# Two zero fills on ScalarE, a third behind the wide patterns, and the wide distances behind the first pattern, in an attention and channel-mix kernel

## The chip, the core and the metric

The kernel runs on one NeuronCore of a Trainium2 chip: TensorE (PE) multiplies matrices, VectorE (DVE), ScalarE (ACT) and GpSimd (POOL) do elementwise work, and SyncE (SP) issues the DMA transfers. The metric is the device time of one launch in microseconds. Before the change it was 506.46 us, the median of three runs (506.25, 506.46 and 509.65).

## What is computed

Attention over 4 batches, 8 heads, 768 positions and 64 features, with a window of `n_local` = 96 keys and `n_global` = 8 keys that all may see, and a linear bias by distance; its output goes through a channel mix of two matrix products and a gate.

```python
scores = (q @ k^T) / sqrt(64) - slope[h] * dist      # slope[h] = 2 ** -(h + 1)
dist   = n_local where the key is global and not local, else |i - j|
a      = softmax(scores where the key is global or local, else -1e9)
x      = a @ v                                       # (4, 768, 512)
xk, xr = mu * x + (1 - mu) * x_prev                  # x_prev: one position earlier
out    = sigmoid(xr @ w_r) * (relu(xk @ w_k) ** 2 @ w_v)
```

## The kernel before

**Tiles.** A tile is 128 queries of one batch, all 8 heads: 24 tiles, 6 per batch. A tile's scores are made two heads at a time (`scores`, hp = 0 to 3, PSUM tiles `s_0` to `s_3`, two buffers). The first tile of a batch sees its own 128 keys. Any other sees 104 earlier keys as well (8 global ones, then the 96 before it), 232 in all. DVE adds the bias pattern to the scores and finds the largest in the same instruction (L366), ACT takes the exponential and its sum (L367), DVE makes the reciprocal (L373, L374), POOL or ACT scales (L380, L378), PE transposes (L392), ACT copies to SBUF (L394), and PE multiplies by v two tiles later in the program (L411).

**The native tiles.** The first six tiles use 128-partition operands of which only the lower 64 partitions hold data; the upper 64 are zeroed once (L261 to L271). There are two query buffers (`qz`) and a ring of three key buffers (`kz`), so five fills of 64x1024 on POOL. Tile 0 needs query 0 and key 0; tile 1 query 1, key 1 and key 0; tile 2 key 2 too. `first_keys` (L274) copies the batch's 8 global keys out of key buffer 0 (`k_first`), and, for tile 1, writes them over a strip of key buffer 0 that tile 1's L357 reads. That write waits until tile 0's scores have read the buffer.

**The patterns.** `pat0` (8 heads of 128x128) is the bias of a batch's first tile, `pat` (8 heads of 128x232) that of all others. Both come from distances that DVE computes from iota values and the two sizes, which a DMA brings: L118 to L128 make `dist0`, the six L132 on DVE and two L134 on POOL scale it per head, L137 to L140 make the wide `dist`, four L144 on ACT and four L146 on POOL scale that. L693 to L698 (`okf`) test whether the sizes fit this path.

**The weights.** Ten slabs of 1 MB come as 64-bit words. DVE packs each to 32 bits (L174 to L176), ACT rounds it to a high half (L178), and for the first six PE makes the rest (L188, L189), which ACT copies (L190). Channel-mix work (`kp`, `z`, `vps`) is fed into the PE stream a few matmuls at a time.

**What sets the order.** Each engine runs its own stream in order. The streams' order is made when the program is built, by a scheduler that simulates a timeline, so an edit to one engine's work can shift neighbours on others. All large loads go through SP's one queue; a load waits there for its buffer, and what stands behind it waits too. Ten matmuls on zeros (L95) stand at the head of PE's stream.

Of the kernel before, what the change touches and what calls it, by code (L numbers as in the profile page):

```python
# [25 lines left out]
GMAX = 8  # L26
# [15 lines left out]
def tile_biased_attention_channel_mix(ctx: ExitStack, tc: tile.TileContext, qT, kT, v, n_sizes, mu_kr, w_k, w_v, w_r, q_rows, k_rows, v_rows, slopes, out):  # L42
# [94 lines left out]
    vec.tensor_scalar(local[:, 0:96], flts[:, 0:96], nlf, FAR, op0=ALU.is_ge, op1=ALU.mult)  # L137
    vec.tensor_copy(dist[:, OWN:W], local[:, 96:224])
    vec.tensor_scalar(dist[:, 0:GMAX], glo[:, 0:GMAX], nlf, None, op0=ALU.max)
    vec.tensor_add(dist[:, GMAX:OWN], local[:, 0:96], flts[:, 0:96])  # L140
    for h in range(H):
        c = -8.0 * 2.0 ** -(h + 1)
        if h % 2:
            act.mul(pat[:, h, :], dist, c)  # L144
        else:
            pool.tensor_scalar(pat[:, h, :], dist, c, 1.0, op0=ALU.mult, op1=ALU.mult)  # L146
# [3 lines left out]
    w_raw, w_live, w_done = {}, {}, {}  # L150

# [6 lines left out]
    def weight_load(i):  # L158


        raw = w_raw[i] = const.tile([128, 1024, 2], I32, tag=f"w{i}", name=f"w64_{i}")
        tc.keep_in_program_order(weight_words(i, raw))

    def weight_begin(i):


        name, src, j = w_steps[i]
        raw = w_raw.pop(i)
        a = p4k.tile([128, 1024], I32, tag="t4k", name=f"wa_{i}")
        low, top = raw[:, :, 0], raw[:, :, 1]  # L170

        vec.tensor_scalar(a, top, 3, 0x3FFFFFF8, op0=ALU.logical_shift_left, op1=ALU.bitwise_and)  # L174
# [3 lines left out]
        act.copy(both[:, 0, :], a.bitcast(F32))  # L178
        w_live[i] = a, both
        w_done[i] = both  # L180

    def weight_end(i):
        name, src, j = w_steps[i]
        a, both = w_live.pop(i)
        if name in 'kr':
            for o in (0, 512):
                rest = ps_f.tile([128, 512], F32, name=f"rest_{i}_{o}", tag="f")
                pe.matmul(rest, ident, a.bitcast(F32)[:, o : o + 512], start=True, stop=False)  # L188
                pe.matmul(rest, minus, both[:, 0, o : o + 512], start=False, stop=True)  # L189
                act.copy(both[:, 1, o : o + 512], rest)  # L190
        else:
            vec.tensor_sub(both[:, 1, :], a.bitcast(F32), both[:, 0, :])
        for k in range(1 if name == "k" else 2):
# [65 lines left out]


    q_zero, k_ring = [], []  # L261
# [12 lines left out]
    def first_keys(n):  # L274
        if n % NT:
            pool_copy(state[n - 1]["kr"][0:64, :, 128 - OWN : 128 - BACK], k_first)
        else:
            pool_copy(k_first, state[n]["kr"][0:64, :, 0:GMAX])

    def load_tile(n):  # L280
# [12 lines left out]
        for o in halves:  # L293
            nc.sync.dma_start(qr[o : o + 64], qT[n])
        for o in halves:
# [9 lines left out]
    def load_v(n):  # L305

        b, t = divmod(n, NT)
        va = v_pool.tile([128, DM], F32, name=f"va_{n}", tag="va")
# [36 lines left out]
    def scores(n, hp):  # L345
# [16 lines left out]
        for u in range(2):  # L362
            h = 2 * hp + u
            o = ps[:, u * 256 : u * 256 + w]
            e = e_pool.tile([128, W], F32, name=f"e_{n}_{h}", tag="e")
            vec.tensor_tensor_reduce(out=e[:, :w], in0=o, in1=p[:, h, :], op0=ALU.add, op1=ALU.min, scale=-0.125, scalar=3.0e38, accum_out=s["nmax"][:, h : h + 1])  # L366
            act.activation(e[:, :w], e[:, :w], AF.Exp, bias=s["nmax"][:, h : h + 1], scale=-1.0, accum_out=s["sum"][:, h : h + 1])  # L367
            s["e"][h] = e
        if hp % 2 == 0:
            return  # L370
# [4 lines left out]
        for u in range(nh):  # L375
            e = s["e"][h0 + u]
            if n < 6 and u < 1:
                act.mul(e[:, :w], e[:, :w], r[:, u : u + 1])  # L378
# [3 lines left out]
    def transposes(n, hp):  # L382
# [10 lines left out]
        for k, p in enumerate(parts):  # L393
            act.copy(et[0:p, k * 256 : k * 256 + 256], pt[0:p, k * 256 : k * 256 + 256])  # L394
        s["et", hp] = et

    def weighted(n, hp):
# [14 lines left out]
        if hp == 3:  # L412
# [8 lines left out]
            xt = state["x", c]  # L421
            act.copy(xt[:, :, 1 + 128 * i : 129 + 128 * i], s["av"].rearrange("p (a q) -> p a q", a=4))  # L422

# [5 lines left out]
    def mix(xc, xp, tag, tmp_pool, out_pool, on_act=False):  # L429
# [9 lines left out]
        act.copy(hi, tmp)  # L439
        vec.tensor_sub(lo, tmp, hi)  # L440
        return hi, lo
# [62 lines left out]
    def ffn(c):  # L504
        xt = state["x", c]
        xk = mix(xt[:, :, 1:257], xt[:, :, 0:256], "k", p4k, f_pool, c == 0)
        xr = mix(xt[:, :, 1:257], xt[:, :, 0:256], "r", p4k, f_pool, c == 0)
# [3 lines left out]
    LAG = 3  # L511
    queue = []
    budget = [0.0]
# [14 lines left out]
    for step in range(NTILES + 1):  # L528
# [6 lines left out]
        for hp in range(4):  # L535
# [9 lines left out]
            if hp == 0:  # L545
                if step >= LAG and (step - LAG) % 2 == 0:
                    queue.append(ffn((step - LAG) // 2))
                    if len(queue) == 1 and step == LAG:
                        budget[0] = -17.5
            run_ffn(2.5)  # L550
# [3 lines left out]
            slot = 4 * step + hp  # L554
            weights_load(W_LOADS[min(slot, len(W_LOADS) - 1)])
            n = W_BEGUN[min(slot, len(W_BEGUN) - 1)]
            weights_go(n, n - 1 if slot < len(W_BEGUN) else n)
    for i in range(4):
# [133 lines left out]
    wide_i = const.tile([1, 1], I32, name="wide_i")  # L692
    vec.tensor_scalar(okf[:, 0:1], nlf, float(LMAX), None, op0=ALU.is_le)  # L693
    vec.tensor_scalar(okf[:, 1:2], nlf, 1.0, None, op0=ALU.is_ge)
    vec.tensor_mul(okf[:, 0:1], okf[:, 0:1], okf[:, 1:2])
    vec.tensor_scalar(okf[:, 1:2], ngf, float(GMAX), None, op0=ALU.is_le)
    vec.tensor_mul(okf[:, 0:1], okf[:, 0:1], okf[:, 1:2])
    vec.tensor_scalar(okf[:, 0:1], okf[:, 0:1], -1.0, 1.0, op0=ALU.mult, op1=ALU.add)  # L698
    vec.scalar_tensor_tensor(okf[0:1, 0:1], worst[0:1, 1:2], 256.0, okf[0:1, 0:1], op0=ALU.is_gt, op1=ALU.max)
# [49 lines left out]
```

## Time and profile before

| | |
|---|---|
| median of three runs | 506.46 us |
| the profiled execution | 507.19 us |
| its span, first to last instruction | 505.4 us |
| PE busy | 495.7 us (98%) |
| DVE, ACT, POOL busy | 352.9, 344.8, 233.1 us |
| mean granted clock of PE | 0.988 of full |

The profile is of one execution. The span leaves out 1.8 us around the program. Times in the rows below are counted from the span's start. A matmul's end is modelled, so PE's waits are best read from where its next instruction starts, and from the view of waits.

### The profile page before, as it was taken

To read this page: it belongs to the slowest core of one execution; us is meant where nothing else is said; L and a number is where in the kernel's file an instruction comes from. 1 tells how busy PE (TensorE), PEld (TensorE's weight loads), DVE (VectorE), ACT (ScalarE), POOL (GpSimd) and SP (SyncE) were. 2 spreads that over 40 slices of the span, in tenths; PEclk is the share of its full clock that TensorE was granted. 3 is DMA by queue.
4 is the path that set the end of the run, shared out by engine and by line. 5 is a ranking of instruction groups with operands and counts; after the bars stand their busy time and mean duration, and the time that the engine had idled before them with its cause. 6 is when DMAs were issued, how large, how long until landed. Compare 5 with 4: busy or idle time off the path is not lost.

```text
span 505.4 us, 10334 instructions
## 1 busy us (share of the span) xinstructions
PE 495.7 (98%) x3608; PEld 435.4 (86%) x3608; DVE 352.9 (70%) x842; ACT 344.8 (68%) x857; POOL 233.1 (46%) x374
## 2 busy tenths in 40 slices
PE   6999999999999999999999999999999999999996
PEld 3767998998998998898898898898898898897985
DVE  6897979968678668658768658758768755457441
ACT  4799878577577577666577677667577678587360
POOL 7552438546546535527547536528447435204000
PEclk8799999999999999999999999999999999999999
DMA  8997361633503603513512513513423215647311
GB/s 240 323 236 252 106 184 38 163 85 83 165 22 92 176 18 85 144 58 79 152 38 82 156 51 80 150 55 81 130 61 79 84 41 163 207 155 263 127 41 48
DMA packets 22586, 60.57 MB, mean 120 GB/s; under 512 B 3296, under 2 KB 4576, under 8 KB 22016
## 3 DMA queue, kind: packets, MB, share of 16 engines
q1 hardware_dynamic: 22384, 59.85, 40.8%
q8 instruction: 30, 0.49, 0.4%
q14 instruction: 28, 0.23, 0.2%
q10 hardware_dynamic: 144, 0.00, 0.0%
HBM read 53.55 MB, written 6.29 MB: 118 GB/s over the span
## 4 chain that ended last, share of the span: by engine, by line
PE 97%; DVE 1%; DMA 1%; issue 0%; POOL 0%; POOLq 0%
PE kp L447 9%; PE kp L449 9%; PE kp L448 9%; PE vps L447 9%; PE vps L449 9%; PE vps L448 9%; PE av L411 9%; PE t L392 9%; PE z L447 5%; PE z L448 4%; PE z L449 4%; PE s L361 3%; PE s L360 3%; PE s L358 3%; PE rest L188 2%; PE s L357 2%
## 5 line engine op out<-in xcount | busy, mean ns | idle before, releaser
L380 POOL TENSOR_SCALAR e<-e,r 128x232 f32<-128x232 f32 (+1 forms) x180 | 94.3, 543 | 151.6 <-DVE r L374 122.6
L447 PE MATMUL kp<-xk_hi,wk 128*128 128x256 f32 x384 | 108.5, 282 | 0.0
L367 ACT ACTIVATE e<-e,nmax 128x232 f32<-128x232 f32 (+1 forms) x192 | 89.9, 471 | 26.3 <-DVE nmax L366 25.7
L449 PE MATMUL kp<-xk_hi,wk 128*128 128x256 f32 x384 | 107.5, 280 | 0.0
L448 PE MATMUL kp<-xk_lo,wk 128*128 128x256 f32 x384 | 107.4, 280 | 0.0
L366 DVE CUSTOM_DVE_ANT_0 e<-s,pat 128x232 f32<-128x232 f32 (+1 forms) x192 | 64.8, 374 | 20.4 <-PE s L361 15.7
L447 PE MATMUL vps<-wv,kk_hi 128*128 128x512 f32 (+1 forms) x200 | 76.6, 384 | 0.0
L449 PE MATMUL vps<-wv,kk_lo 128*128 128x512 f32 (+1 forms) x200 | 76.6, 383 | 0.0
L448 PE MATMUL vps<-wv,kk_hi 128*128 128x512 f32 (+1 forms) x200 | 76.4, 382 | 0.0
L448 PEld LDWEIGHTS kp<-xk_lo,wk 128*128 128x128 f32 x384 | 72.1, 188 | 0.6 <-issue 0.2
L447 PEld LDWEIGHTS kp<-xk_hi,wk 128*128 128x128 f32 x384 | 72.2, 188 | 0.4
L449 PEld LDWEIGHTS kp<-xk_hi,wk 128*128 128x128 f32 x384 | 72.1, 188 | 0.1
L394 ACT COPY et<-t 128x256 f32<-128x256 f32 (+1 forms) x176 | 56.8, 372 | 9.7 <-PE t L392 8.7
L475 DVE TENSOR_TENSOR kk<-kp,kk 128x512 f32<-128x512 f32 x48 | 33.0, 688 | 40.4 <-ACT kk L474 40.1
L392 PE MATMUL t<-ident,e 128*128 128x128 f32 x352 | 56.0, 279 | 0.0
L477 DVE TENSOR_TENSOR kk_lo<-kk,kk_hi 128x512 fp32r<-128x512 f32 x48 | 34.9, 726 | 23.0 <-ACT kk_hi L476 22.6
L392 PEld LDWEIGHTS t<-ident,e 128*128 128x128 f32 x352 | 41.0, 137 | 11.0 <-issue 2.4
L336 DVE TENSOR_TENSOR ql<-qraw,qh 128x1024 fp32r<-128x1024 f32 x18 | 35.9, 1997 | 12.3 <-POOL qh L255 12.3
L449 PEld LDWEIGHTS vps<-wv,kk_lo 128*128 128x128 f32 x200 | 37.6, 188 | 7.4
L447 PEld LDWEIGHTS vps<-wv,kk_hi 128*128 128x128 f32 x200 | 37.7, 189 | 6.6 <-issue 0.2
L448 PEld LDWEIGHTS vps<-wv,kk_hi 128*128 128x128 f32 x200 | 37.7, 189 | 6.3
L422 ACT COPY x<-av 128x512 f32<-128x512 f32 x24 | 14.1, 587 | 40.7 <-PE av L411 40.7
(113 smaller groups left out, 1118.5 us busy)
## 6 DMA issues: line engine op xcount, KB each, us to landing
qraw<-in_qT_dram SPq DMA_DIRECT2D x36, 256.0 KB
kraw<-in_kT_dram SPq DMA_DIRECT2D x36, 256.0 KB
out_dram<-sig SPq DMA_DIRECT2D x23, 256.0 KB
va<-in_v_dram SPq DMA_DIRECT2D x20, 240.0 KB
vb<-in_v_dram SPq DMA_DIRECT2D x20, 208.0 KB
w<-in_w_k_dram SPq DMA_DIRECT2D x4, 1024.0 KB
w<-in_w_v_dram SPq DMA_DIRECT2D x4, 1024.0 KB
again<-in_w_k_dram SPq DMA_DIRECT2D x8, 512.0 KB
```

The source lines that it names most:

```text
L336: vec.tensor_sub(ql, s["qr"], qh)
L366: vec.tensor_tensor_reduce(out=e[:, :w], in0=o, in1=p[:, h, :], op0=ALU.add, op1=ALU.min, scale=-0.125, scalar=3.0e38, accum_out=s["nmax"] ...
L367: act.activation(e[:, :w], e[:, :w], AF.Exp, bias=s["nmax"][:, h : h + 1], scale=-1.0, accum_out=s["sum"][:, h : h + 1])
L380: pool.tensor_scalar(e[:, :w], e[:, :w], r[:, u : u + 1], 1.0, op0=ALU.mult, op1=ALU.mult)
L392: pe.transpose(pt[0:p, c : c + 128], e[:, k * 128 : k * 128 + p], ident)
L394: act.copy(et[0:p, k * 256 : k * 256 + 256], pt[0:p, k * 256 : k * 256 + 256])
L411: pe.matmul(o, vt[:, h * 64 : (h + 1) * 64], et[0:p, c + q : c + 128], start=k == 0, stop=k == nb - 1)
L447: pe.matmul(o, sh, mh, start=first, stop=False)
L448: pe.matmul(o, sh, ml, start=False, stop=False)
L449: pe.matmul(o, sl, mh, start=False, stop=last)
L475: vec.tensor_mul(kk, pv, kk)
L477: rest = vec.tensor_sub(kkl[:, 2 * fp : 2 * fp + 2, :], kk, kkh[:, 2 * fp : 2 * fp + 2, :])
```

## The change

The fills of the upper halves get a table. Query 1 and key 1 are zeroed by ACT, each as two copies of 64x512 from a tile of zeros. Key 2 stays on POOL but is issued behind the last wide pattern that POOL makes. Query 0 and key 0 are as before. Of the narrow patterns, head 6 goes to ACT and head 7 to DVE; both were POOL's. The four DVE instructions that make the wide distances are issued behind the last narrow pattern of DVE. The other entries of the table repeat what the code before did.

```diff
+PLAN = {
...
+    "Z": {('q', 1): 'A', ('k', 1): 'A', ('k', 2): 'L'},
+    "P0": 'DDDDDDAD',
+    "GD": 1,
...
     for h in range(H):
         c = -8.0 * 2.0 ** -(h + 1)
-        if h < 6:
-            vec.tensor_scalar(pat0[:, h, :], dist0, c, None, op0=ALU.mult)
+        if PLAN.get("P0", "DDDDDDPP")[h] == "A":
+            act.mul(pat0[:, h, :], dist0, c)
+        elif PLAN.get("P0", "DDDDDDPP")[h] == "D":
+            first_done = vec.tensor_scalar(pat0[:, h, :], dist0, c, None, op0=ALU.mult)
         else:
             pool.tensor_scalar(pat0[:, h, :], dist0, c, 1.0, op0=ALU.mult, op1=ALU.mult)
...
+        if PLAN.get("GD"):
+            later.enter_context(tc.issue_after(first_done.ins))
+        vec.tensor_scalar(local[:, 0:96], flts[:, 0:96], nlf, FAR, op0=ALU.is_ge, op1=ALU.mult)
+        vec.tensor_copy(dist[:, OWN:W], local[:, 96:224])
+        vec.tensor_scalar(dist[:, 0:GMAX], glo[:, 0:GMAX], nlf, None, op0=ALU.max)
+        vec.tensor_add(dist[:, GMAX:OWN], local[:, 0:96], flts[:, 0:96])
...
+    def zero_half(which, i, half):
+        e = PLAN.get("Z", {}).get((which, i), "P")
+        if e == "P":
+            pool.memset(half, 0.0)
+        elif e == "A":
+            for h in (0, 4):
+                act.copy(half[:, h : h + 4, :], zeros[64:128].rearrange("p (h q) -> p h q", h=4))
...
+        else:
+            with tc.issue_after(pattern_done.ins):
+                pool.memset(half, 0.0)
...
-            pool.memset(q_zero[i][64:128], 0.0)
+            zero_half("q", i, q_zero[i][64:128])
...
-        pool.memset(kz[64:128], 0.0)
+        zero_half("k", i, kz[64:128])
```

On DVE, between the distances and the first bias (`btmp` holds all distances, `pat_137` is the narrow pattern, `e_0` the first head of tile 0; most rows of `okf` and those that read out a largest value are left out), the order was:

```order
L126 TENSOR_SCALAR btmp<-btmp,sizes 128x128
L137 TENSOR_SCALAR btmp<-btmp,sizes 128x96
L693 TENSOR_SCALAR okf<-sizes 128x1
L127 TENSOR_TENSOR btmp<-btmp 128x128
L139 TENSOR_SCALAR btmp<-btmp,sizes 128x8
L140 TENSOR_TENSOR btmp<-btmp 128x96
L128 SCALAR_TENSOR_TENSOR btmp<-btmp,sizes 128x128
L138 COPY btmp<-btmp 128x128
L132 TENSOR_SCALAR pat_137<-btmp 128x128 x6
L697 TENSOR_TENSOR okf<-okf 128x1
L366 ISA e_0_201,nmax_192<-s_0_198,pat_137 128x128
```

and is now (lines are the changed kernel's):

```order
L147 TENSOR_SCALAR btmp<-btmp,sizes 128x128
L148 TENSOR_TENSOR btmp<-btmp 128x128
L149 SCALAR_TENSOR_TENSOR btmp<-btmp,sizes 128x128
L155 TENSOR_SCALAR pat_137<-btmp 128x128 x7
L163 TENSOR_SCALAR btmp<-btmp,sizes 128x96
L164 COPY btmp<-btmp 128x128
L165 TENSOR_SCALAR btmp<-btmp,sizes 128x8
L771 TENSOR_TENSOR okf<-okf 128x1
L433 ISA e_0_203,nmax_194<-s_0_200,pat_137 128x128
L433 ISA e_1_206,nmax_194<-s_0_200,pat_137 128x128
L166 TENSOR_TENSOR btmp<-btmp 128x96
```

Seven patterns stand where six did, three of the four wide distance steps stand between them and the first bias, and the fourth (L140 before, L166 now) behind the second bias.

On POOL, from the fills to the strip that tile 1 reads (`kz_179`, `kz_183`, and `kz_186` or now `kz_188` are key buffers 0, 1 and 2), the order was:

```order
L267 MEMSET qz_178 64x1024
L270 MEMSET kz_179 64x1024
L267 MEMSET qz_182 64x1024
L270 MEMSET kz_183 64x1024
L270 MEMSET kz_186 64x1024
L255 TENSOR_SCALAR k_first<-kz_179 64x64
L134 TENSOR_SCALAR pat_137<-btmp 128x128 x2
L146 TENSOR_SCALAR pat<-btmp 128x232 x4
L255 TENSOR_SCALAR kz_179<-k_first 64x8x8
```

and is now:

```order
L308 MEMSET qz_178 64x1024
L308 MEMSET kz_179 64x1024
L297 TENSOR_SCALAR k_first<-kz_179 64x64
L172 TENSOR_SCALAR pat<-btmp 128x232 x4
L318 MEMSET kz_188 64x1024
L297 TENSOR_SCALAR kz_179<-k_first 64x8x8
```

The third key fill now stands directly ahead of the write of the strip.

On ACT the four copies stand between the table load and the first product, and the wide patterns (L170) behind the first two exponentials of tile 0 instead of ahead of them:

```order
L311 ACT_TABLE_LOAD
L311 CAST qz_182<-zeros 64x512 x2
L311 CAST kz_183<-zeros 64x512 x2
L85 ACTIVATE minus<-ident 128x128
L153 ACTIVATE pat_137<-btmp 128x128
L434 ACTIVATE e_0_203,sum_193<-e_0_203,nmax_194 128x128
L434 ACTIVATE e_1_206,sum_193<-e_1_206,nmax_194 128x128
L170 ACTIVATE pat<-btmp 128x232 x4
L434 ACTIVATE e_2_222,sum_193<-e_2_222,nmax_194 128x128
```

Before, ACT ran the table load, `minus`, the four wide patterns and then the eight exponentials. The scheduler also re-sorts all engines' streams over the first tiles and slabs; SP's order is the same row for row.

## Rows read from the trace of the kernel before

**Rows 1.** The page: the span, PE's busy time, the chain's shares.
```profile
span 505.4 us, 10334 instructions
...
PE 97%; DVE 1%; DMA 1%; issue 0%; POOL 0%; POOLq 0%
```
**Rows 2.** Waits of PE: waited for, us in total, times, longest.
```profile
PE s L358 <- DVE nmax L366: 1.8, 1, 1.8
PE s L358 <- DMA va<-in_v_dram: 1.4, 1, 1.4
...
PE s L357 <- POOL kz L255: 0.5, 1, 0.5
```
**Rows 3.** Timeline of PE: start, us, engine, line, operation, [idle before, releaser].
```profile
6.52 1.13 PE L358 MATMUL s<-kz,qz 128*128 128x128 f32 x8 [1.43 <-DMA va<-in_v_dram]
...
9.66 2.07 PE L358 MATMUL s<-kz,qz 128*128 128x128 f32 x8 [1.80 <-DVE nmax L366]
12.19 0.76 PE L357 MATMUL s<-kz,qz 128*128 128x104 f32 x2 [0.46 <-POOL kz L255]
```
**Rows 4.** Windows: length; busy PE, PEld, DVE, ACT, POOL; clock; DMA; GB/s.
```profile
8.00:9.00 1.00, 0.00 (x0) 0.00 (x0) 1.00 (x6) 0.91 (x4) 0.84 (x3) 0.62 1.14 338
9.00:18.00 9.00, 7.85 (x34) 6.60 (x34) 6.86 (x33) 6.19 (x26) 4.77 (x10) 0.50 1.03 330
18.00:19.00 1.00, 1.00 (x8) 0.49 (x7) 0.81 (x2) 0.72 (x3) 0.00 (x0) 0.76 1.01 266
40.00:60.00 20.00, 20.00 (x145) 15.72 (x144) 17.03 (x43) 19.61 (x52) 6.03 (x8) 1.00 0.50 172
```
**Rows 5.** Timeline of DVE from the sizes to the first two biases.
```profile
4.12 0.62 DVE L57 CAST words<-sizes_w 128x4 f32<-128x4 int32 x1 [2.07 <-DMA sizes_w<-in_n_sizes_dram]
...
4.77 0.16 DVE L58 SCALAR_TENSOR_TENSOR sizes<-words 128x2 f32<-128x2 f32 x1
4.85 0.28 DVE L121 TENSOR_TENSOR btmp<-btmp 128x128 f32<-128x128 f32 x1
...
5.24 0.53 DVE L125 TENSOR_SCALAR btmp<-btmp,sizes 128x128 f32<-128x128 f32 x1
...
5.76 1.03 DVE L137 TENSOR_SCALAR btmp<-btmp,sizes 128x96 f32<-128x96 f32 x1
...
6.83 0.26 DVE L140 TENSOR_TENSOR btmp<-btmp 128x96 f32<-128x96 f32 x1
...
7.41 0.21 DVE L138 COPY btmp<-btmp 128x128 f32<-128x128 f32 x1
...
7.61 1.32 DVE L132 TENSOR_SCALAR pat<-btmp 128x128 bf16<-128x128 f32 x6
...
9.11 0.28 DVE L366 CUSTOM_DVE_ANT_0 e<-s,pat 128x128 f32<-128x128 f32 x1
```
**Rows 6.** Timeline of POOL: second to fifth fill, then wide patterns and strip.
```profile
3.77 0.94 POOL L267 MEMSET qz<- 64x1024 f32 x1
4.66 1.04 POOL L270 MEMSET kz<- 64x1024 f32 x1
...
5.63 1.09 POOL L270 MEMSET kz<- 64x1024 f32 x1
...
8.33 1.65 POOL L146 TENSOR_SCALAR pat<-btmp 128x232 bf16<-128x232 f32 x4
11.90 0.24 POOL L255 TENSOR_SCALAR kz<-k_first 64x64 f32<-64x64 f32 x1 [1.92 <-PE s L358]
```
**Rows 7.** Timeline of ACT: table load, wide patterns, the eighth exponential.
```profile
1.17 1.28 ACT L64 ACT_TABLE_LOAD   x1 [1.17 <-PEq L739]
...
7.66 1.25 ACT L144 ACTIVATE pat<-btmp 128x232 bf16<-128x232 f32 x4 [4.88 <-DVE btmp L138]
...
12.62 0.38 ACT L367 ACTIVATE e<-e,nmax 128x128 f32<-128x128 f32 x1
```
**Rows 8.** The page: ACT's copy of 128x512: busy, mean ns, idle before.
```profile
L422 ACT COPY x<-av 128x512 f32<-128x512 f32 x24 | 14.1, 587 | 40.7 <-PE av L411 40.7
```

More of the change, by code (lines that the diff above doesn't have):

```diff
@@ L161, in weight_load @@
         raw = w_raw[i] = const.tile([128, 1024, 2], I32, tag=f"w{i}", name=f"w64_{i}")
-        tc.keep_in_program_order(weight_words(i, raw))
+        with ExitStack() as later:
+            g = PLAN.get("WB", {}).get(i)
+            if g in q_load:
+                later.enter_context(tc.issue_after(q_load[g].ins))
+            tc.keep_in_program_order(weight_words(i, raw))
     def weight_begin(i):
@@ L170, in weight_begin @@
         low, top = raw[:, :, 0], raw[:, :, 1]
-        vec.tensor_scalar(a, top, 3, 0x3FFFFFF8, op0=ALU.logical_shift_left, op1=ALU.bitwise_and)
+        with ExitStack() as later:
+            g = PLAN.get("BEHIND", {}).get(i)
+            if g in biased:
+                later.enter_context(tc.issue_after(biased[g].ins))
+            if isinstance(g, int) and g < len(mixed):
+                later.enter_context(tc.issue_after(mixed[g].ins))
+            vec.tensor_scalar(a, top, 3, 0x3FFFFFF8, op0=ALU.logical_shift_left, op1=ALU.bitwise_and)
         vec.scalar_tensor_tensor(a, top, -0x40000000, a, op0=ALU.bitwise_and, op1=ALU.bitwise_or)
@@ L177, in weight_begin @@
         both = const.tile([128, 2, 1024], F32R, tag=f"w{i}", name=f"w{name}{j}")
-        act.copy(both[:, 0, :], a.bitcast(F32))
+        hi_engine = PLAN.get("HI", "AAAAAAAAAA")[i]
+        if hi_engine == "A":
+            act.copy(both[:, 0, :], a.bitcast(F32))
+        elif hi_engine == "P":
+            pool_copy(both[:, 0, :], a.bitcast(F32))
+        else:
+            vec.tensor_copy(both[:, 0, :], a.bitcast(F32))
         w_live[i] = a, both
@@ L189, in weight_end @@
                 pe.matmul(rest, minus, both[:, 0, o : o + 512], start=False, stop=True)
-                act.copy(both[:, 1, o : o + 512], rest)
+                (vec.tensor_copy if PLAN.get("RC", "A" * 20)[2 * i + o // 512] == "D" else act.copy)(both[:, 1, o : o + 512], rest)
         else:
-            vec.tensor_sub(both[:, 1, :], a.bitcast(F32), both[:, 0, :])
+            (pool if PLAN.get("LOW", "PPPPPPDDDD")[i] == "G" else vec).tensor_sub(both[:, 1, :], a.bitcast(F32), both[:, 0, :])
         for k in range(1 if name == "k" else 2):
@@ L258, in tile_biased_attention_channel_mix @@
     state = {}
+    held = []
+    def zero_half(which, i, half):
[5 more added lines that the diff above has]
+                act.copy(half[:, h : h + 4, :], zeros[64:128].rearrange("p (h q) -> p h q", h=4))
+        elif e == "D":
+            vec.memset(half, 0.0)
+        elif e == "H":
+            held.append(half)
+        else:
+            with tc.issue_after(pattern_done.ins):
+                pool.memset(half, 0.0)
     q_zero, k_ring = [], []
@@ L305, in load_v, with load_v_now @@
     def load_v(n):
+        g = PLAN.get("VB", {}).get(n)
+        if g in q_load:
+            with tc.issue_after(q_load[g].ins):
+                load_v_now(n)
+        else:
+            load_v_now(n)
+    def load_v_now(n):
         b, t = divmod(n, NT)
@@ L365, in scores @@
             e = e_pool.tile([128, W], F32, name=f"e_{n}_{h}", tag="e")
-            vec.tensor_tensor_reduce(out=e[:, :w], in0=o, in1=p[:, h, :], op0=ALU.add, op1=ALU.min, scale=-0.125, scalar=3.0e38, accum_out=s["nmax"][:, h : h + 1])
+            biased[n, hp] = vec.tensor_tensor_reduce(out=e[:, :w], in0=o, in1=p[:, h, :], op0=ALU.add, op1=ALU.min, scale=-0.125, scalar=3.0e38, accum_out=s["nmax"][:, h : h + 1])
             act.activation(e[:, :w], e[:, :w], AF.Exp, bias=s["nmax"][:, h : h + 1], scale=-1.0, accum_out=s["sum"][:, h : h + 1])
             s["e"][h] = e
+        while held and hp == 3:
+            with tc.issue_after(biased[n, hp].ins):
+                vec.memset(held.pop(), 0.0)
         if hp % 2 == 0:
@@ L376, in scores @@
             e = s["e"][h0 + u]
-            if n < 6 and u < 1:
+            if (n, hp, u) in PLAN["ER"]:
                 act.mul(e[:, :w], e[:, :w], r[:, u : u + 1])
@@ L393, in transposes @@
         for k, p in enumerate(parts):
-            act.copy(et[0:p, k * 256 : k * 256 + 256], pt[0:p, k * 256 : k * 256 + 256])
+            (vec.tensor_copy if (n, hp, k) in PLAN.get("ET", ()) else act.copy)(et[0:p, k * 256 : k * 256 + 256], pt[0:p, k * 256 : k * 256 + 256])
         s["et", hp] = et
@@ L439, in mix @@
         act.copy(hi, tmp)
-        vec.tensor_sub(lo, tmp, hi)
+        mixed.append(vec.tensor_sub(lo, tmp, hi))
         return hi, lo
@@ L692, in tile_biased_attention_channel_mix @@
     wide_i = const.tile([1, 1], I32, name="wide_i")
[L693 to L698, printed above, removed]
+    with ExitStack() as later:
+        if PLAN.get("GO"):
+            later.enter_context(tc.issue_after(biased[K["GO"]].ins))
+        vec.tensor_scalar(okf[:, 0:1], nlf, float(LMAX), None, op0=ALU.is_le)
+        vec.tensor_scalar(okf[:, 1:2], nlf, 1.0, None, op0=ALU.is_ge)
+        vec.tensor_mul(okf[:, 0:1], okf[:, 0:1], okf[:, 1:2])
+        vec.tensor_scalar(okf[:, 1:2], ngf, float(GMAX), None, op0=ALU.is_le)
+        vec.tensor_mul(okf[:, 0:1], okf[:, 0:1], okf[:, 1:2])
+        vec.tensor_scalar(okf[:, 0:1], okf[:, 0:1], -1.0, 1.0, op0=ALU.mult, op1=ALU.add)
     vec.scalar_tensor_tensor(okf[0:1, 0:1], worst[0:1, 1:2], 256.0, okf[0:1, 0:1], op0=ALU.is_gt, op1=ALU.max)
```

48 lines of the change are left out of this document (31 added, 17 removed).

## The prediction

> **What bounds the kernel now.** The page comes first: PE is on the chain that ended last for 97% of a span of 505.4 us [rows 1]. The view of PE's waits comes second: behind the matmuls on zeros it lists three, 1.4, 1.8 and 0.5 us, and none after them [rows 2]. The timeline of PE says where they lie [rows 3]. At 6.52 the first two score tiles of tile 0 start. The other two start only at 9.66, because a PSUM buffer comes free when DVE has added the bias and found the largest value. Tile 1 starts at 12.19, when POOL has written the strip of key buffer 0. From there PE is never listed as idle, so the end moves with the moment the stream gets going, and with the clock it gets. Third, the windows [rows 4]: the granted clock is 0.62 in the mean of 8 to 9 us, 0.50 from 9 to 18, and 0.76 in the mean of 18 to 19. So it fell to its lower level (1.2 of 2.4 GHz) near 8.2 and came back near 18.5. Up to 12.19 that costs little, since PE waits much of that time; from 12.19 to 18.5 PE streams at half speed. The last of these windows, 40 to 60 us, shows ACT busy for 19.6 of 20 us and DVE for 17.0: a head start of PE must be shared by them to last.
>
> **Why the first bias is late.** The first bias (L366) starts at 9.11 [rows 5]. Ahead of it three DVE instructions last far longer than their size explains. L57 converts four elements in 0.62 us and ends at 4.74; POOL's second-buffer query fill ends at 3.77 + 0.94 = 4.71. L125 ends at 5.77, the key fill at 4.66 + 1.04 = 5.70. L137 ends at 6.79, the third key fill at 5.63 + 1.09 = 6.72 [rows 5, 6]. Three holds end within 0.1 us behind the end of a fill: these are the fills that the change takes off POOL at that hour.
>
> **The change, part by part.**
>
> *Fills of query 1 and key 1 on ACT.* Four copies of 64x512. Nearest row: ACT's copy of 128x512, 0.59 us each [rows 8], so 2.4 us. The table load ends at 2.45, and ACT then has little to do until 7.66; it is listed 4.88 us idle there [rows 7]. The copies end near 4.8, `minus` near 5.1, and tile 1 reads the buffers behind 11. Cost nothing; without that cover it would be up to 2.4 us on ACT.
>
> *The holds on DVE.* An L58 takes 0.16, so L57's hold is 0.46. A copy of 128x128 takes 0.21 (L138), so L125's is 0.32 and L137's 0.82 [rows 5]. All three gone: 1.60. The lower end is 0.82, if the two small ones only moved waiting that the chain has anyway.
>
> On these holds the Trainium skill, "SBUF — State Buffer", section "Who interferes with whom", has a rule: GpSimd and VectorE share a port pair, which copies, casts and `tensor_scalar` in their fast modes take whole; whichever starts first shuts the other out, while an instruction with two SBUF inputs is shut out only by a GpSimd one that reads. By the rule all three held ones (a cast and two `tensor_scalar`) are of the kind that a fill stops, and the sum would take 1.60; by the rows alone it lies between 0.82 and 1.60. The trace agrees so far: L121, with two inputs, lasted 0.28 in the middle of a fill [rows 5, 6].
>
> *The wide distances.* Between the last narrow pattern and the first bias now stand L137, L138 and L139, and L140 behind the second bias. So only L140 leaves the path to the first bias (0.26 at most); for the narrow patterns the whole group is out of the way, but the first bias waits for it as before. One narrow pattern more on DVE: 1.32 / 6 = 0.22 [rows 5]. These two cancel.
>
> First bias: 0.6 to 1.6 us earlier. The low end is 0.82 less the new pattern, the high end all three holds. I take 1.3, nearer the high end, because each of the three rows ends where a fill ends: 9.11 becomes 7.8. The scores it needs are there, since PE starts them at 6.52 and needs 1.13 for both tiles [rows 3]. PE's second pair of score tiles follows at 9.66 - 1.3 = 8.4 and, with its 2.07, is done at 10.45.
>
> *Wide patterns and the third key fill.* The wide distances are complete behind L140: 7.8 + two biases (0.28 each at most) + 0.26 = 8.6 with the start of L140, against about 7.6 before (L138 ends at 7.62). So POOL's wide patterns start at 8.6, where before it was 8.33, and end at 8.6 + 1.65 = 10.2. Now the third fill, 0.94 to 1.09 [rows 6], stands between them and the strip: 11.2. Before, POOL sat idle 1.92 us ahead of the strip, waiting for PE's tile 0; now PE's tile 0 is done at 10.45 and waits for POOL. The strip's write started at 11.90 and PE followed at 12.19, 0.29 later [rows 3, 6]. So tile 1 starts at 11.2 + 0.29 = 11.5, 0.7 us earlier than 12.19. Ends: 1.45 earlier if POOL is ready when tile 0 is done (10.75), and 0 if the first bias gains only 0.6 (9.3 + 1.65 + 1.05 + 0.29 = 12.3). The fill that was made to wait thus takes back half of the head start.
>
> *ACT's order.* One narrow pattern more (a wide one takes 1.25 / 4 = 0.31) lies ahead of the first bias, beside DVE. The wide patterns stand behind the second exponential: 7.8 + 0.3 for the first, two at 0.38, then 1.25, then six at 0.38 end at 12.4, where before the eighth ended at 13.0 [rows 7]. No loss.
>
> *The rest.* Two narrow patterns leave POOL. No DMA is added and SP's order is unchanged. PE does the same products in another order: for tile 0 the last two transposes are behind tile 1's scores and the first slab's rest, which spares PE a wait for late heads; I count nothing for it.
>
> **Sum.** Tile 1 and all behind it start 0.7 us earlier. If PE alone paced the stretch to 18.5, and the clock came back when it did, the 0.7 at half clock would be worth 0.35 at full; if PE there waits for exponentials, which also come earlier, all 0.7. I take 0.7, since DVE (1.3) and ACT (0.6) are ahead as well. Against its own time the profiled execution goes from 507.19 to 506.5. That execution is 0.73 above the median of the three runs, so the median goes from 506.46 to **505.8 us**. Of this case alone: 505.0 to 506.2.
>
> **Rivals.**
>
> *The fill eats it all.* If the holds give only their low end, tile 1 starts at 12.2 as before and the end is unchanged: 506.4. For it: the DVE chain ahead of 7.6 has write-to-read gaps that no fill causes. Against it: three coincidences with fills.
>
> *Slower: the slow clock comes later and covers more work.* PE now waits about 1.0 us, from 10.45 to 11.5, just ahead of its dense stream, while its earlier wait shrinks by 1.3, from 1.80 to 0.5. If the clock holds through 8.2 and falls at this new wait instead, for as long as before (10.3 us), it lies over 11.5 to 21.8, all streaming. PE then does 5.15 us worth of full-clock work by 21.8. Before, from 12.19, it did 6.3 / 2 + 3.3 = 6.45. That is 1.3 more than lost before: 507.7. It decides when the windows show clock 1.00 in 9 to 10 and 0.50 in 19 to 21. For it: the fall near 8.2 followed gaps of 1.43 and 1.80, and one of these shrinks. Against it: 1.0 us is shorter than either.
>
> The Trainium skill, "TensorE: Matmul & The Clock Gate", Part 1, says that the lower clock is the default and activity lifts it, and that the point of change shifts by about 500 ns from run to run. By it this rival and the next can differ between runs of one kernel, 507.7 or 504.1; no row of one execution shows that.
>
> *Faster: the clock comes back sooner.* With the stream going from 11.5, it might return at 15 in place of 18.5: 3.5 us at half clock, 1.7 us back, 504.1. Against it: from 12.19 PE streamed without a listed wait and the clock still took until 18.5.
>
> **How the numbers follow.** Forecast 0.50 (505.8); the fill eats it 0.20 (506.4); slow clock later 0.17 (507.7); clock back sooner 0.13 (504.1). The range takes in the first three and most of the last, with 0.1 us beyond each end: 503.8 to 507.9. About 1%, 5 us, is what a measurement can tell from no change here. All four cases lie inside it: the two removable waits are 2.3 us together and the half clock over 12.19 to 18.5 costs 3.2, so 5 us faster would need nearly all. Slower by 5 us needs a stall in the re-sorted streams that no row points to. Faster 0.02, within 1% 0.95, slower 0.03.
>
> **What would show it.** Right: no DVE instruction between the sizes and the first bias above 0.4 us; first bias near 7.8; the strip's write directly behind a POOL fill, near 11.2; PE's wait for POOL grown from 0.46 to about 1.0, its wait for DVE gone to 0.5 or less; tile 1 near 11.5. The hold step is wrong if L57 or L125 still lasts 0.5 or more; the POOL step if PE's wait for the strip is not longer than before; the sum if tile 1 starts near 11.5 and PE's stream at 60 us is not ahead. A half-clock stretch at another place makes a rival right.

## The result, and the profile after

| | before | after |
|---|---|---|
| median (lowest to highest) of 11 runs each, taken together | 507.17 us (505.27 to 509.65) | 510.19 us (506.90 to 511.47) |
| ratio to before, 95% interval | | 1.0057 (1.0037 to 1.0076) |
| runs of 509.5 us or more | 1 of 11 | 7 of 11 |
| the profiled execution, its span | 507.19, 505.4 us | 510.62, 508.8 us |

The change made the kernel 0.6% slower: 3.0 us between the medians, 3.4 between the two spans. The forecast was 0.7 us faster, with a range that ended at 507.9.

The head of the program went as forecast. First DVE in the changed kernel (timeline: start, us, engine, line, operation, [idle before, releaser]), which answers to [rows 5]:

```profile
4.08 0.20 DVE L78 CAST words<-sizes_w 128x4 f32<-128x4 int32 x1 [2.08 <-DMA sizes_w<-in_n_sizes_dram]
...
4.84 0.29 DVE L146 TENSOR_SCALAR btmp<-btmp,sizes 128x128 f32<-128x128 f32 x1
...
6.07 1.09 DVE L155 TENSOR_SCALAR pat<-btmp 128x128 bf16<-128x128 f32 x7
7.08 0.26 DVE L163 TENSOR_SCALAR btmp<-btmp,sizes 128x96 f32<-128x96 f32 x1
...
7.73 0.29 DVE L433 CUSTOM_DVE_ANT_0 e<-s,pat 128x128 f32<-128x128 f32 x1
```

No instruction ahead of the first bias is held any more (L78, L146 and L163 are the three that were: L57, L125 and L137), and that bias starts at 7.73. POOL, for [rows 6], then PE, for [rows 3]:

```profile
8.49 1.64 POOL L172 TENSOR_SCALAR pat<-btmp 128x232 bf16<-128x232 f32 x4 [1.82 <-DVE okf L772]
10.20 0.95 POOL L318 MEMSET kz<- 64x1024 f32 x1
11.22 0.24 POOL L297 TENSOR_SCALAR kz<-k_first 64x64 f32<-64x64 f32 x1
```
```profile
6.50 2.05 PE L425 MATMUL s<-kz,qz 128*128 128x128 f32 x8 [1.28 <-DMA va<-in_v_dram]
...
8.76 1.49 PE L425 MATMUL s<-kz,qz 128*128 128x128 f32 x8
11.51 0.47 PE L424 MATMUL s<-kz,qz 128*128 128x104 f32 x2 [1.26 <-POOL kz L297]
...
36.96 0.72 PE L424 MATMUL s<-kz,qz 128*128 128x104 f32 x2 [2.66 <-DMA qz<-in_qT_dram]
```

Tile 1 starts at 11.51, behind the moved fill and the strip. The last row is new: at 36.96 PE has waited 2.66 us for the load of tile 3's query. In [rows 2] there is no such wait. The windows (columns as in [rows 4]):

```profile
9.00:18.00 9.00, 7.50 (x55) 6.17 (x55) 7.46 (x32) 7.86 (x30) 5.05 (x11) 1.00 1.04 332
...
33.00:37.00 4.00, 1.34 (x5) 0.45 (x4) 3.04 (x7) 3.28 (x12) 0.61 (x2) 1.00 0.94 187
37.00:43.00 6.00, 6.00 (x25) 4.58 (x26) 2.69 (x8) 3.12 (x7) 1.32 (x3) 0.50 0.06 17
43.00:45.00 2.00, 2.00 (x10) 0.78 (x9) 0.00 (x0) 0.38 (x1) 0.00 (x0) 0.80 0.00 0
```

From about 9.6 us PE ran at its upper level and did 55 products by 18 us, where before it did 34 at the lower one [rows 4]. By an estimate from the columns of all matmul records, PE had by 34 us done about 3.4 us (at the full clock) more than before: a larger head start than forecast, and nearly all of it was there by 18.5 us, when the low clock of the execution before ended. Then it stood still, and behind the wait its clock was 0.50 to about 43.8. At 44 us it was, by the same estimate, about 2.2 us behind. The DMA column falls to 0.06, DVE and ACT to about half: all idle together. From 30 to 36.9 us the share is 0.96 in the changed kernel, and it was as high before:

```profile
30.00:36.90 6.90, 6.90 (x46) 4.18 (x45) 6.34 (x15) 6.54 (x19) 3.24 (x4) 1.00 0.97 189
```

The chain of waits has an entry that was not there before, "DMA qz<-in_qT_dram 3.6%". A milestone late enough to tell the end, the first product with a slab of `w_v`, before and after:

```profile
78.62 0.39 PE L447 MATMUL vps<-wv,kk_hi 128*128 128x512 f32 x1
```
```profile
82.11 0.40 PE L517 MATMUL vps<-wv,kk_hi 128*128 128x512 f32 x1
```

It is 3.5 us later, about as the end is (3.4): the loss lies ahead of it.

**Two theories.** *Supply*: PE's head start carries it past what the loads have brought; the wait and the half clock behind it cost more than was won. *Order*: the scheduler re-sorted the streams of PE, DVE and ACT behind the opening, and that loses the time, whatever loads and clock do. Two places stand out in the order. On PE, before, all sixteen products with v of tile 1 stood ahead of tile 3's first scores; now eight stand behind them. On DVE, before, slab 5's first step, which waits for the slab, stood behind tile 2's last two biases; now it stands ahead of them.

### The profile page after: what moved, and what is told of

It reads as the page before. It is cut to its first block, busy times and chain, and to the rows that moved or that the text cites. A ratio compares the mean times of both kernels' runs of the same rounds, so it can differ in the third digit from the quotient of the medians.

```text
span 508.8 us, 10338 instructions
## 1 busy us (share of the span) xinstructions
PE 497.5 (98%) x3608; PEld 436.1 (86%) x3608; DVE 351.8 (69%) x843; ACT 346.7 (68%) x862; POOL 222.4 (44%) x370
## 4 chain that ended last, share of the span: by engine, by line
PE 93%; DMA 4%; SPq 1%; POOL 1%; DVE 0%; issue 0%; ACT 0%
PE kp L517 9%; PE kp L519 9%; PE kp L518 9%; PE vps L517 9%; PE vps L519 9%; PE vps L518 9%; PE av L481 8%; PE t L462 8%; PE z L517 5%; PE z L519 4%; PE z L518 4%; DMA qz<-in_qT_dram 4%; PE s L428 3%; PE s L427 3%; PE s L425 2%; PE s L424 2%
## 5 line engine op out<-in xcount | busy, mean ns | idle before, releaser
L450 POOL TENSOR_SCALAR e<-e,r 128x232 f32<-128x232 f32 (+1 forms) x180 | 87.4, 503 | 165.8 <-DVE r L444 121.9
L462 PE MATMUL t<-ident,e 128*128 128x128 f32 x352 | 54.9, 276 | 0.0
```

The costliest lines, as they stand in the source:

```text
L450: pool.tensor_scalar(e[:, :w], e[:, :w], r[:, u : u + 1], 1.0, op0=ALU.mult, op1=ALU.mult)
L462: pe.transpose(pt[0:p, c : c + 128], e[:, k * 128 : k * 128 + p], ident)
```

## The experiments

In most kernels the streams of PE, DVE and ACT were held in a chosen order, so that an edit could not re-sort them:

```diff
+        for engine, packed in HELD.items():     # ranks in the order that is wanted
+            mine = [i for i in traced if i.engine == engine]
...
+            for a, b in zip(ranks, ranks[1:]):
+                tc.add_manual_dep(mine[b], mine[a].name, ...)
```

Times are medians beside the kernel before on the same chip; n is the number of runs. A ratio is to the kernel before, with its 95% interval; it takes all runs, and differs from the quotient of the two medians by up to 0.0012.

### Opening and order, crossed

> The change's opening (fills, patterns, wide distances) with the streams of PE, DVE and ACT behind tile 0's exponentials held in the order of the kernel before. Supply theory (the changed kernel's full early clock carries PE some 3 us ahead of the loads, PE waits 2.7 us for tile 3's query at 34.3 to 37.0, and the clock falls behind that wait): PE comes to tile 3's scores near 36 instead of 38.9, the query lands at 36.8 to 37.2, so a wait of 0.5 to 1.5 us; if the clock falls again behind it 509 to 510.5, if it holds 506 to 507.5. Order theory (the re-sorted streams lose the time, whatever clock and loads do): the loss is gone and the head start is kept, 504 to 506.5.

> The opening of the kernel before with the streams of PE, DVE and ACT held in the order of the changed kernel. Supply theory: the early stretch at half clock is back, PE is not ahead of the loads, its wait for tile 3's query is under 0.5 us, no half clock near 37 us, 506.5 to 508. Order theory: as slow as the changed kernel, 509.5 to 511.

| | old streams | new streams |
|---|---|---|
| old opening | 1 (before) | 1.0028 (1.0007 to 1.0050), 508.62 against 507.69, n = 12 |
| new opening | 0.9985 (0.9967 to 1.0003), 507.07 against 507.69, n = 12 | 1.0057 (1.0037 to 1.0076) (after) |

The same opening is 0.7% apart between the two orders. So the order is needed for the loss; supply alone is not enough. But the order alone costs half of it. With the old opening the new order's profile shows the same wait, shorter, since PE comes later:

```profile
37.26 0.44 PE L364 MATMUL s<-kz,qz 128*128 128x104 f32 x2 [0.67 <-DMA qz<-in_qT_dram]
```

### The wait taken away, and filled

```diff
+            if n == 3 and h < 7:
+                q_in, k_in = (w_done[0][:, j, h * 128 : h * 128 + 128].bitcast(F32) for j in (0, 1))
```

> The changed kernel, all streams in its order; seven of the eight heads of tile 3's scores are made of the first weight slab instead of tile 3's query and key (the same number and size of products; the loads stay), so PE need not wait for that load at 34.3 us. Supply theory: no wait for the query, the clock stays at its upper level at 37 to 44 us, and of the 2.7 us of waiting and the 3.4 us of half clock most comes back: 504 to 506. Order theory: the order is the same, so the time is too, 509.5 to 511 (or 507.5 if the wait alone comes back).

506.03 against 507.69 (n = 12), ratio 0.9974 (0.9954 to 0.9993), as the supply theory had it. The order is the changed kernel's, and without that one wait it is faster than before: span 503.5 us. PE comes to the scores of tile 3 at 34.88 and does not stop, and the first product with `w_v` starts at 76.81:

```profile
34.88 0.36 PE L431 MATMUL s<-kz,wk 128*128 128x104 f32 x2
...
76.81 0.40 PE L528 MATMUL vps<-wv,kk_hi 128*128 128x512 f32 x1
```

This is the strongest single result: in the new order the query's wait, with what follows from it, is the whole loss and more.

```diff
+        for i in range(12 if (n, hp) == (3, 0) else 0):
+            pe.matmul(ps, zeros[:, 0:128], zeros, start=True, stop=True)
```

> The changed kernel, all streams in its order, with twelve matmuls on zeros (128x512 bf16, 213 ns each at the full clock, 2.6 us) ahead of tile 3's scores, where PE waits 2.66 us for the query. The wait is filled, not removed. Supply theory: the clock no longer falls at 37 us and the 3.4 us that half clock cost come back: 506 to 507.5, with tile 3's scores at 37.0 as before. Order theory, or a clock that falls whatever PE does there: 510 to 511.

511.58 against 507.69 (n = 9), ratio 1.0084 (1.0054 to 1.0115): a miss, and a useful one. Its profiled execution (509.76 us, span 508.0, the second fastest of the nine) did what was meant, but for one thing: the zeros ran from 35.14, the clock stayed up, and tile 3's scores followed at 37.74, so the zeros themselves held PE up by about 0.8 us against the 36.96 of the changed kernel:

```profile
35.14 2.76 PE L427 MATMUL s<-zeros 128*128 128x512 bf16 x11
37.74 0.36 PE L433 MATMUL s<-kz,qz 128*128 128x104 f32 x2
...
55.99 0.44 PE L433 MATMUL s<-kz,qz 128*128 128x104 f32 x2 [1.47 <-DVE nmax L442]
```
```profile
36.90:44.00 7.10, 7.10 (x49) 4.76 (x48) 3.49 (x9) 5.27 (x13) 1.53 (x4) 1.00 0.16 42
```

Yet its first product with `w_v` comes at 81.19. DVE (3.49 of 7.10 us) and the DMA queue (0.16) starve at full clock too, and PE meets the late DVE at 55.99. So the half clock is not needed for the loss. That it cost 3.4 us of its own does not fit either: without it the first product with `w_v` comes 0.9 us earlier than the 82.11 of the changed kernel, or 1.7 with the 0.8 added, an estimate from two single executions.

### The query ahead of slab 5, and slab 5's step behind

```diff
-    "WB": {},
+    "WB": {5: 3},
```

In query_first slab 5's first step on DVE goes behind two biases as well, as in the DVE diff further down.

> The changed kernel, PE and ACT in its order; in SP's queue tile 3's key and query are moved ahead of the sixth slab (slab 5), and slab 5's first step on DVE, which waits for that slab, is moved behind tile 2's last two biases. Supply theory (PE reaches tile 3's scores near 34.3 us, before the query lands at 36.8, and the clock falls behind that wait): the query lands a slab earlier, near 33.5, PE's wait for it is under 0.5 us, the clock holds at 37 to 44: 504.5 to 506.5. Order theory (PE's re-sorted stream loses the time by itself): 509.5 to 511; with only the wait given back, 507.5.

> The change's opening with PE, DVE and ACT in the order of the kernel before (507.07 as measured), and tile 3's key and query ahead of slab 5 in SP's queue. Supply theory: in executions whose clock rises early PE stands 2 to 3 us ahead at 34 us and no longer runs into the query: 505 to 506.5. Order theory: the load's place does not matter, 506.8 to 507.4.

511.44 against 507.15 (n = 6), ratio 1.0082 (1.0055 to 1.0109), and 510.03 (n = 4), 1.0057 (1.0040 to 1.0075). Both miss, and teach most: the wait did not go, it moved. PE of the first, then of the second:

```profile
34.23 1.13 PE L237 MATMUL rest<-wa,ident 128*128 128x512 f32 x2 [1.02 <-DVE wa L219]
41.24 1.12 PE L237 MATMUL rest<-wa,ident 128*128 128x512 f32 x2 [1.44 <-DVE wa L219]
```
```profile
42.26 1.72 PE L237 MATMUL rest<-wa,ident 128*128 128x512 f32 x2 [2.90 <-DVE wa L219]
```

PE now waits for DVE's last step (L219) on slab 3 and on slab 4; in the second kernel on slab 4 alone. In DVE's stream these stand behind the first step (L217) on the next slab, which waits for its load. DVE of the first kernel: the first step on slab 4 and the last on slab 3, then the first on slab 5 and the last on slab 4:

```profile
32.35 0.69 DVE L217 TENSOR_SCALAR wa<-w 128x1024 int32<-128x1024 int32 x1 [2.88 <-DMA w<-in_w_r_dram]
32.96 1.22 DVE L219 SCALAR_TENSOR_TENSOR wa<-w,wa 128x1024 int32<-128x1024 int32 x1
...
39.36 0.69 DVE L217 TENSOR_SCALAR wa<-w 128x1024 int32<-128x1024 int32 x1 [3.28 <-DMA w<-in_w_r_dram]
39.97 1.22 DVE L219 SCALAR_TENSOR_TENSOR wa<-w,wa 128x1024 int32<-128x1024 int32 x1
```

The DMA share is about 1 up to 37 us in either kernel, so a load moved up moves another back, and DVE's order hands that wait on to PE. Whether the query first would pay with those last steps ahead of the next slab's first one was not run.

```diff
-TENSOR_SCALAR wa<-w_5 128x1024
 ISA e_6,nmax<-s_3,pat 128x232
 ISA e_7,nmax<-s_3,pat 128x232
+TENSOR_SCALAR wa<-w_5 128x1024
```

(`e_6` and `e_7` are tile 2's last two biases.)

> The changed kernel with one step moved: slab 5's first step on DVE, which waited 1.84 us for the slab with tile 2's last two biases behind it, goes behind them; all else, SP's queue too, in the changed kernel's order. Supply theory: tile 3's query lands as before and PE still waits for it, 509.5 to 511. A theory that the loss sits in DVE's order, in the two biases held up behind the slab: 508 to 509.

508.57 against 507.15 (n = 6), ratio 1.0039 (1.0015 to 1.0063): between the two, and not resolved from the changed kernel. Its profiled run, of 511.11 us, has the query's wait (2.70 at 37.04) and the half clock. So the step alone does not cure it.

### Less to load, and a colder start

```diff
+        return nc.sync.dma_start(raw[:, 0:64, :], src[j * 256 : j * 256 + 128, 0:128]...)
```

> The changed kernel, PE, DVE and ACT in its order; slab 5's load brings 64 KB in place of 1 MB (the rest of the slab is filled with zeros by GpSimd near 22 us, where it is idle, so the gate's matrix is wrong by that slab), and tile 3's query and key go ahead of it. Nothing that comes later than 1 MB less of loading is waited for. Supply theory, in its wider form (by 37 us PE needs the whole of the first loads, query and slab 5 alike, so putting one ahead of the other only moves the wait): no wait of 0.5 us or more for the query or for slab 4 or 5 between 30 and 45 us, the clock holds, 504 to 506.5. Order theory: 509.5 to 511.

> The same cut of slab 5's load in the kernel before, streams in its own order. Supply theory: PE comes to tile 3's scores after the query in any case, so the missing megabyte is worth little there: 506.3 to 507.5, at most half of what it gives the changed kernel. If the loads limit both kernels alike: 504 to 505.5. Order theory says nothing of it.

507.57 against 506.85 (n = 12), ratio 1.0017 (0.9994 to 1.0039), and 506.48 (n = 12), 0.9995 (0.9973 to 1.0018). The direction is the supply theory's: nearly a megabyte less in slab 5 is worth 0.4% to the changed kernel and nothing measurable to the one before. The size is a miss for the changed kernel: 504 to 506.5 was expected. Its profile lists no wait of PE behind tile 1's start at 11.32; why it is still slower than no_wait, no run shows.

> The changed kernel with slabs 4 and 5 (the gate's matrix) loaded behind tile 3's query, the streams free to be made anew, so that PE's and DVE's work on these slabs moves back too. Supply theory: tile 3's scores wait for nothing, and PE has tiles 3 and 4 to go on with while the slabs come: 505 to 507 if the new streams put the slabs' work late enough, 509 to 511 if PE runs into slab 4 or 5 instead. Order theory: it is another order, so nothing is said.

507.26 against 506.85 (n = 12), ratio 1.0005 (0.9981 to 1.0030), 0.3 us above the first range. The diff is `"WB": {4: 3, 5: 3}`; no wait for the query is left, and a new one of 1.51 us for DVE at 54.64.

```diff
-    for i in range(10):
+    for i in range(4):
```

> The changed kernel, streams in its order, with four matmuls on zeros at the head of PE's stream in place of ten (PE does nothing from about 3 us to 6.5). Supply theory: the clock rises later, PE is not ahead of the loads and waits less than 1 us for tile 3's query, with no half clock near 37 us: 507.5 to 509, faster than the changed kernel although its start is colder. If an early clock only helps: 511 to 513. Order theory: 510 to 511.

510.49 against 507.15 (n = 6, 507.92 to 515.41), 1.0068 (1.0031 to 1.0105). Inconclusive: in its queue tile 2's query stood behind slab 2, and its profile shows PE waiting 2.62 us for that at 23.05.

> The changed kernel unchanged, for a second profile of it. Supply theory: in an execution of 507 to 508 the clock rises later than 9.6 us or falls near 11 us, PE has no wait over 1 us for tile 3's query and no half clock near 37 us; in one of 510 to 511.5 the wait and the half clock are there again. Order theory: the place of the loss does not depend on the clock.

509.61 us, one run, between the two groups. The clock fell at 12.15, behind the wait near 11 us; PE still waited for the query, and no half clock followed:

```profile
11.30 0.47 PE L424 MATMUL s<-kz,qz 128*128 128x104 f32 x2 [1.85 <-POOL kz L297]
...
37.12 0.44 PE L424 MATMUL s<-kz,qz 128*128 128x104 f32 x2 [2.02 <-DMA qz<-in_qT_dram]
...
71.92 0.50 PE L517 MATMUL z<-wr,xr_hi 128*128 128x512 f32 x1 [1.93 <-DVE kk L545]
```

As in the kernel with the zeros, PE pays at DVE later: 1.93 us at 71.92. The first product with `w_v` comes at 81.12, 2.5 us behind the kernel before, though no half clock followed the wait.

### The two places turned

```diff
-MATMUL s_0<-kz,qz ...   (tile 3: seven products, here and between the next rows)
 MATMUL av<-et_2,va ...  (tile 1: eight products)
 MATMUL rest<-wa,ident ... (slab 4: two)
 MATMUL t<-ident,e ...   (tile 2: eight)
+MATMUL s_0<-kz,qz ...   (the seven)
```

> The changed kernel with one piece of PE's stream turned: tile 3's first seven score products go behind the eight products with v of tile 1, the two of slab 4 and tile 2's first eight transposes, which stood behind them (about 2.7 us of PE's work at the full clock); DVE and ACT in the changed kernel's order. Order and supply together (the new streams put tile 3's scores ahead of work that needs no load, so PE stands before the query while it could do that work): the wait for the query is under 0.7 us in every execution, the times of 510 and above vanish, 506 to 507.5. Supply alone (PE comes to the end of what is loaded in any order): 509 to 511 as in the changed kernel, with the wait at the query, or at slab 5.

508.08 against 507.39 (n = 12, none over 509.31), ratio 1.0008 (0.9992 to 1.0024). The times of 510 and above are gone as expected, but the median is above the 506 to 507.5 that was expected: the wait for the query is gone, and a shorter one for DVE's last step on slab 4 stands in its place:

```profile
37.05 1.13 PE L237 MATMUL rest<-wa,ident 128*128 128x512 f32 x2 [1.33 <-DVE wa L219]
```

> The changed kernel with both pieces of its order turned: tile 3's first score products on PE behind the work that needs no load, and slab 5's first step on DVE behind tile 2's last two biases. If these two pieces are the order's whole share of the loss, the time is that of the opening in the old order: 506.5 to 507.5, no execution at 510. If the slab's step on DVE is nothing, as with the first piece alone: 508. If the loads take the head start back in any order: 509 to 511.

507.24 against 506.57 (n = 12, none over 508.03), ratio 1.0001 (0.9984 to 1.0018). The first place takes back 0.49 of the 0.57%; the second adds 0.07, which is not resolved. This profile is a twin of the changed kernel's: PE's last product of slab 3 starts at 33.50 there and 33.51 here. Then (PE of both_pieces):

```profile
33.51 0.80 PE L238 MATMUL rest<-wk,minus 128*128 128x512 f32 x1
34.24 0.45 PE L488 MATMUL av<-et,va 128*64 128x128 f32 x4
...
35.87 1.13 PE L237 MATMUL rest<-wa,ident 128*128 128x512 f32 x2 [0.80 <-DVE wa L219]
...
39.27 0.37 PE L431 MATMUL s<-kz,qz 128*128 128x104 f32 x2
```

The work that does not need the query fills the time to its landing, but for 0.80 us of waiting for slab 4's last step. Three windows of the same stretch, before, after and both_pieces:

```profile
36.90:44.00 7.10, 7.10 (x49) 5.35 (x48) 6.35 (x16) 6.19 (x14) 2.60 (x4) 1.00 0.67 226
```
```profile
36.90:44.00 7.10, 7.04 (x28) 4.68 (x28) 2.79 (x8) 3.22 (x7) 1.32 (x3) 0.52 0.06 16
```
```profile
36.90:44.00 7.10, 6.97 (x46) 5.19 (x45) 3.47 (x16) 3.05 (x8) 1.21 (x3) 1.00 0.75 243
44.00:60.00 16.00, 15.12 (x122) 12.97 (x122) 13.82 (x32) 16.00 (x45) 3.90 (x9) 1.00 0.56 180
```

28 products against 46 and 49, and the queue, which waits for buffers that those products free, at 0.06 against 0.75. The last row shows where a part of PE's head start goes in both_pieces: ACT, which stood half idle ahead of 44 us, is busy 16.00 of 16.00 us behind it, and PE stands idle for 0.88 of them, 0.57 in a wait for ACT at 44.60. Where the rest goes is not shown; the first product with `w_v` starts at 79.00, 0.4 behind the kernel before.

### The third fill behind the strip, and the best order

```diff
-    "Z": {('q', 1): 'A', ('k', 1): 'A', ('k', 2): 'L'},
+    "Z": {('q', 1): 'A', ('k', 1): 'A', ('k', 2): 'S'},
...
+        while late and (n, hp) == (0, 1):
+            with tc.issue_after(scaled.ins):
+                pool.memset(late.pop(), 0.0)
```

> The changed kernel, PE, DVE and ACT in its order; the third key fill on GpSimd goes behind the strip and tile 0's first three scalings, so that PE's wait for the strip (1.26 to 1.87 us near 11 us) shrinks to 0.5 us or less. By the prediction's sum it would be worth the 0.8 us or more that the fill took back: 509.5. Supply theory: PE is only further ahead at 34 us and waits longer for the query, 510 to 512, no gain; the half clock that follows the wait near 11 us is gone.

> Both of the two: tile 3's scores behind the work that needs no load, and the third key fill behind the strip. Order and supply together: 505.5 to 507, PE further ahead than with the first alone but with some wait for the query or slab 5 again. Supply alone: 510 to 512.

> The change's opening with PE, DVE and ACT in the order of the kernel before, and the third key fill behind the strip. If the wait for the strip near 11 us and the half clock behind it cost what they seem to, and the old streams leave PE room ahead of the query: 505 to 506.5, under the kernel before. If the loads take it back: 506.5 to 508.

fill_late: 510.49 against 507.39 (n = 11), 1.0064 (1.0043 to 1.0085). Tile 1 starts at 10.65 in place of 11.51, but the wait at the query is as long as before (2.64 against 2.66) and ends only 0.26 us earlier:

```profile
10.65 0.47 PE L433 MATMUL s<-kz,qz 128*128 128x104 f32 x2 [0.45 <-DVE nmax L442]
...
36.70 0.55 PE L433 MATMUL s<-kz,qz 128*128 128x104 f32 x2 [2.64 <-DMA qz<-in_qT_dram]
```

PE loses most of the 0.86 us on the way, 0.55 of it in a wait for ACT at 13.90. With the scores behind: 507.67 (n = 12), 1.0007 (0.9989 to 1.0026). In the old order: 506.64 (n = 12), 0.9982 (0.9964 to 1.0000). In the old order tile 1 starts at 10.23 in place of 11.36 (after_old_order), and PE then waits 1.91 us for ACT at 15.03. None of the three differs from its kernel without the edit (1.0064 and 1.0057, 1.0007 and 1.0008, 0.9982 and 0.9985). The fill that was "taking back half" shows no worth, though intervals of 0.2% to either side would hide 0.7 us in any one pair.

> The change's opening with the third key fill behind the strip; PE, DVE and ACT in the changed kernel's order up to the first scores of tile 2, and from there in the order of the kernel before. Order and supply together: the changed order of the first 20 us leaves out PE's wait of 1.9 us at tile 0's transposes that the old order has near 15 us, and the old order behind it has work ahead of tile 3's query: 505.5 to 506.8, under the kernel before. Supply alone: what PE is ahead at 30 us is lost at the query, 506.6 as without the changed order, or slower.

506.33 against 506.57 (n = 12, 505.16 to 506.76), ratio 0.9984 (0.9968 to 0.9999). It is the one version with all its computation whose interval lies below 1, and barely: the medians are 0.24 us apart, and with so many versions run one such interval can be chance. That it is 0.7% under the changed kernel is clear. Its query wait is 0.81 us at 36.87, its first product with `w_v` at 77.97.

## Why the prediction was wrong

- **The holds, ACT's copies, the wide distances: right.** First bias 7.73 (7.8 forecast), L78 at 0.20 where L57 took 0.62. The four copies took 2.26 us (2.4) and delayed nothing: the eighth exponential ends at 12.3 (12.4). With the fills gone all three holds are gone: 0.62, 0.53 and 1.03 us became 0.20, 0.29 and 0.26. The Trainium skill ("SBUF — State Buffer", section "Who interferes with whom") has GpSimd and VectorE shut each other out at a shared port pair, where casts and `tensor_scalar` take it whole. The trace agrees.
- **POOL and tile 1: right.** Fill at 10.20 (10.2), strip at 11.22 (11.2), tile 1 at 11.51 (11.5), PE's wait 1.26 (1.0).
- **The sum: wrong by its own sign.** It was to be wrong "if tile 1 starts near 11.5 and PE's stream at 60 us is not ahead"; tile 1 started at 11.51, and the first product with `w_v` came 3.5 us later than before. In the old streams the opening did move the median from 507.69 to 507.07, by 0.62 us where 0.66 was forecast, but the interval (0.9967 to 1.0003) includes no change, so the agreement may be luck. Nor is it shown that "the end moves with the moment the stream gets going": old_fill started tile 1 another 1.1 us earlier, and the end did not move.
- **"The rest": the step that failed.** "PE does the same products in another order [...] I count nothing for it." The order costs 0.28% with the old opening and 0.72% (1.0057 against 0.9985) with the new, and the seven products that scores_behind puts back make 0.49 (0.25 to either side) of the 0.57% that the changed kernel lost. In the order that the prediction counted at nothing, tile 3's scores stand ahead of work that does not need their load, and PE, early, waits 2.66 us for it; with that wait taken away (no_wait) the ratio is 0.9974. The order of the streams was there to be read, and was not asked which load each instruction waits for.
- **"A stall in the re-sorted streams that no row points to": a row hinted at it.** The DMA column of [rows 4] is 1.03 and 1.01 from 9 to 19 us; only the clock beside it was read. It stays so to the query's landing: before, it is 0.97 from 30 to 36.9 us. A PE brought forward over that stretch could meet a load, and in the new order did.
- **The rivals.** "Slow clock later" named the kind of mishap, a wait and then half clock, but put it at 11.5; in the profile it came at 36.97. "Clock back sooner" did come in that execution: from 9 to 18 us the clock was at its upper level. It gave no gain, since PE then stood before the query. So both rivals lacked the loads.

What stays open: how much the half clock added in the executions that had it, the share of the second place, why a wait brings the clock down in one place and not in another (below), and what the four runs of the changed kernel at 506.90 to 508.08 lack, since both of its profiles are of slower ones.

## What to carry to other kernels

In this kernel an early gain was worth only what the next resource could follow: read the DMA column where PE is to arrive sooner, and ask of each moved instruction which load it waits for and what needs no load and stands behind it. Where a scheduler re-sorts streams, hold the old order once with the edit in it; that separates the edit's worth from the order's. Moving a load up on a full queue here moved the wait to the load that it passed.

## What the runs showed that was not expected

- **The query's landing barely moves.** In the six profiles where PE waited for it, the wait ended between 36.70 and 37.26 us, whenever PE came: in order of size 36.70, 36.87, 36.96, 37.04, 37.12 and 37.26.
- **The first rise of the clock differs between executions of one kernel.** In the changed kernel's two profiles eight equal products from 6.5 us took 2.05 us in one and 1.13 in the other. The clock column reads 1.00 in both: it holds only changes, so the level at the start is read from the spacing of equal products, as before in [rows 3]. In the first of these the upper level begins at 9.66, in the second PE was at it by 6.7, and in before_new_order only near 17 us. The Trainium skill ("TensorE: Matmul & The Clock Gate", Part 1) has the point of change shift by about 500 ns from run to run. These traces agree that it shifts, but by some 3 us between the two executions, and the measurement decides.
- **A wait may bring the clock down behind it.** It fell within 0.6 us of the end of waits of 2.64, 2.66, 2.70 and 2.90 us at 37 to 42, and at 10.8 to 12.7 around waits of 1.85 to 1.87 in eight profiles; it fell at 37.3, 0.75 us behind one of 1.67 (scores_behind_fill), but not behind 2.02 at 37 (after_again). The Trainium skill ("TensorE: Matmul & The Clock Gate", section "HAM oscillation — how this bites in real kernels") describes a DMA wait after which the work starts at the lower clock; the changed kernel's profile agrees, at 0.50 from 36.97 to about 43.8.
